# Two linear-attention branches with a gate: where x^T of the first 512 rows comes from, and where the gate is applied

## The chip, the core and the metric

The kernel runs on one core of a Trainium2 chip. The metric is device time in microseconds (us), as the median of several executions. A profile of one execution comes with it. Its engines are PE (TensorE: matmuls, and PEld its weight loads), DVE (VectorE), ACT (ScalarE), POOL (GpSimd) and SP, which here only issues DMAs.

## What is computed

Two attention branches A and B read the same x (2048 rows, 640 columns, 32 heads of 20), each with its own weights. A gate per row, from x and one vector, mixes them. Shapes and casts are left out:

```python
def branch(x, wqkv, wo):
    q, k, v = heads(x @ wqkv)
    phi = lambda t: jnp.where(t > 0, t + 1, jnp.exp(t)) + 1e-6
    pq, pk = phi(q), phi(k)
    kv = jnp.einsum("bhsd,bhse->bhde", pk, v)
    z = jnp.einsum("bhsd->bhd", pk)
    num = jnp.einsum("bhqd,bhde->bhqe", pq, kv)
    den = jnp.einsum("bhqd,bhd->bhq", pq, z)[..., None] + 1e-6
    return rows(num / den) @ wo

g = sigmoid((x * gate_w).sum(-1, keepdims=True))
out = g * branch(x, A_wqkv, A_wo) + (1 - g) * branch(x, B_wqkv, B_wo)
```

## The kernel before

The rows are cut into 16 tiles of 128, or 4 blocks of 512. x^T (tile XT, 640 columns as 5 chunks of 128 partitions) stands in SBUF, and so does x itself (XN, with a column of ones behind its 640 columns).

The work goes in stages. First k: for each row tile and branch, ten matmuls of 320 columns (`k_part`, XT against WK), then exp on ACT and two steps on DVE (`phi_k`) that leave phi(k). Then G = phi(k)^T [x | 1], 32 matmuls for each of five column groups and each branch (`g_unit`). ACT copies each G tile out, and SP transposes it by DMA (GTA, GTB). From G, WV and WO come small per-head matrices (`m_unit`) and the product with wo, WP (`wp_unit`, `wp_rows`). Then q: per block and branch five groups of five 512-column matmuls (`q_unit`) and the phi steps. `scale_q` makes the denominators of a block with twenty 32-wide matmuls of 256 columns, four of them side by side in the array (two halves of each branch), adds epsilon on DVE (DN, line 733), takes the reciprocal (RC), writes it to DRAM and reads it back repeated over the rows (RX), and multiplies phi(q) by it on DVE (line 757). Last, `final` multiplies phi(q) by WP: per row tile ten 320-column matmuls for A and ten for B.

The gate is applied in `final`. `gates` (line 654) takes sixteen products of x with the broadcast gate vector on DVE with a running sum (line 659), then exp on ACT, plus one and reciprocal on DVE: GA holds g and 1 - g for each row. In `final`, A's two PSUM banks are copied by ACT with scale g into TS (line 805), and DVE multiplies B's by 1 - g and adds TS (line 811). The last row tile is done in three column parts (320, 160, 160).

The order on each engine is made when the program is built: every operation has an estimated duration and its reads and writes, and `_Sched` places them one after the other on the engine that is free first, by order of writing among those that can start within 20 ns. DMAs stand in the queue of the engine that issues them, in the order in which they are written. `at[0]` chains the first matmuls, so that TensorE keeps their written order.

At the head, x^T of the first block is not loaded: rows 0 to 511 of x come as four loads of 128 rows, TensorE transposes each in five 128x128 steps with an identity that POOL builds (`transpose_x`, lines 472 to 482), and DVE copies the result to XT (line 486). Around them stand warm-up matmuls on ones, whose results nobody reads (`warm`: seven, then one after each of the first stretches). wk of A comes in five loads. ACT's queue issues wk chunks 0, 1, 2, 4 and x tile 3; SP's queue x tiles 0, 1, wk chunk 3, x tile 2, three loads of B's wk, then the DMA transposes of blocks 1 to 3 of x (512 rows each), the constants, the gate vector, x of blocks 1 to 3, and the other weights:

```python
load_wk("ACT", 0)
load_x("SP", 0)
load_wk("ACT", 1)
load_x("SP", 1)
load_wk("ACT", 2)
load_wk("SP", 3)
load_wk("ACT", 4)
load_x("SP", 2)
load_x("ACT", 3)
```

In the profile all matmuls but the transposes have line 396 (helper `mms`), and all DMAs line 385 (helper `dma`).

Of the kernel before, what the change touches and what calls it, by code (L numbers as in the profile page):

```python
# [14 lines left out]
dt = mybir.dt  # L15
# [4 lines left out]
D = 640  # L20
# [8 lines left out]
XW = 672  # L29
# [286 lines left out]
def bass_gated_mix__linear_attn_block__linear_attn_block__prompt_kernel(nc, A_x, A_wqkv, A_wo, B_x, B_wqkv, B_wo, gate_w, out):  # L316
# [6 lines left out]
    with ExitStack() as es:  # L323
# [24 lines left out]
        GL = sb("GL", [128, NT], dt.float32)  # L348
        GE = sb("GE", [128, 2, NT], dt.float32)
        GA = sb("GA", [128, 2, NT], dt.float32)  # L350
        GP = sb("GP", [128, D])
        GWB = sb("GWB", [128, D])
        NTS = 3
        TS = sb("TS", [128, NTS, D], dt.float32)
# [8 lines left out]
        IDN = sb("IDN", [128, 128])  # L363
# [40 lines left out]
        def wsrc(X, lo):  # L404
            return weights(X, lo, 0, NC)


        sch.op("POOL", lambda e: e.memset(IDN[:, :], 0.0), 150, writes=[("ID",)], name="id0")
        sch.op(
            "POOL",  # L410
            lambda e: e.affine_select(
                IDN[:, :], IDN[:, :], pattern=[[-1, 128]], compare_op=ALU.not_equal, fill=1.0, base=0, channel_multiplier=1
            ),
            400, writes=[("ID",)], name="id1",
        )
        def load_x(eng, t):
            dma(eng, "xn%d" % t, XN[:, t, 0:D], xin[128 * t : 128 * t + 128, :], writes=[("XN", t)], us=0.25)

        def load_wk(eng, c):
            dma(eng, "wkA%d" % c, WK["A"][:, c, :], weights("A", D, c, c + 1)[:, 0, :], writes=[("WK", "A", c)], us=0.25)  # L420

        load_wk("ACT", 0)
        load_x("SP", 0)
        load_wk("ACT", 1)
        load_x("SP", 1)
        load_wk("ACT", 2)
        load_wk("SP", 3)
        load_wk("ACT", 4)
        load_x("SP", 2)
        load_x("ACT", 3)  # L430
        for c0, c1 in ((0, 1), (1, 3), (3, 5)):
            dma(
                "SP", "wkB%d" % c0, WK["B"][:, c0:c1, :], weights("B", D, c0, c1), writes=[("WK", "B", c) for c in range(c0, c1)],
                us=0.55 * (c1 - c0),
            )
# [6 lines left out]
        dma("SP", "gw", GWB[:, :], gate_w.partition_broadcast(128), writes=[("GWB",)], us=0.4)  # L442
        for b in range(1, NB):
            dma(
                "SP", "xn_%d" % b, XN[:, 4 * b : 4 * b + 4, 0:D],
                xin[512 * b : 512 * b + 512, :].rearrange("(t p) f -> p t f", p=128),
                writes=[("XN", t) for t in range(4 * b, 4 * b + 4)], us=2.0,
            )
# [22 lines left out]

        def transpose_x(t):
            tt = _Tile(1)

            def fn(pe):
                ins = None
                for c in range(NC):
                    ins = pe.transpose(PSB[:, tt.banks[0], 128 * c : 128 * c + 128], XN[:, t, 128 * c : 128 * c + 128], IDN[:, :])  # L478
                return ins

            at[0] = sch.op(
                "PE", fn, 5 * 112, reads=[("XN", t), ("ID",)], writes=[(tt,)], name="xpose%d" % t, lat=190, after=at[0]
            )
            sch.op(
                "DVE",
                lambda e: e.tensor_copy(
                    XT[:, :, 128 * t : 128 * t + 128], PSB[:, tt.banks[0], 0:D].rearrange("p (c f) -> p c f", f=128)
                ),
                _dve_ns(D), reads=[(tt,)], writes=[("XT", t)], name="xev%d" % t,
            )  # L490

        ring = {"ek": _Ring(NEK), "dn": _Ring(2), "rx": _Ring(2), "os": _Ring(NOS), "ts": _Ring(NTS)}

# [160 lines left out]
        def gates():  # L654

            for t in range(NT):
                sch.op(
                    "DVE",
                    lambda e, t=t: e.scalar_tensor_tensor(  # L659
                        out=GP[:, :], in0=XN[:, t, 0:D], scalar=1.0, in1=GWB[:, :], op0=ALU.mult, op1=ALU.mult, accum_out=GL[:, t : t + 1]  # L660
                    ),
                    _dve_ns(D), reads=[("XN", t), ("GWB",)], writes=[("GL", t), ("GP",)], name="gl%d" % t,
                    after=gone["A"],
                )
            for x, sg in ((0, -1.0), (1, 1.0)):
                sch.op(
                    "ACT", lambda e, x=x, sg=sg: e.activation(GE[:, x, :], GL[:, :], ACT.Exp, scale=sg), _act_ns(NT, False),
                    reads=[("GL", t) for t in range(NT)], writes=[("GE", x)], name="ge%d" % x,
                )
            sch.op(  # L670
                "DVE", lambda e: e.tensor_scalar(GE[:, :, :], GE[:, :, :], 1.0, None, op0=ALU.add), 110, reads=[("GE", 0), ("GE", 1)],
                writes=[("GE", 0), ("GE", 1)], name="ge1",
            )
            sch.op(
                "DVE", lambda e: e.reciprocal(GA[:, :, :], GE[:, :, :]), 330, reads=[("GE", 0), ("GE", 1)], writes=[("GA",)], name="ga",
            )
# [35 lines left out]
        def scale_q(b, pieces):  # L712
# [4 lines left out]
            def den():  # L717
# [15 lines left out]
                lambda e: e.tensor_scalar(DN[:, ds.slot, :], PS[:, dtile.banks[0], 0:256], EPS, None, op0=ALU.add), _dve_ns(256),  # L733
                reads=[(dtile,)], writes=[(ds,)], name="dn%d" % b,
# [33 lines left out]
        def final(t, parts=((0, D),), put=None):  # L768

            last = len(parts) > 1  # L770
            os = None if last else _Tile(1, ring["os"])
            row = out[0, 128 * t : 128 * t + 128, :]
            for lo, hi in parts:
                n = 1 if hi - lo <= 512 else 2
                w = (hi - lo) // n
                ts = _Tile(1, ring["ts"])

                def o_ap(lo=lo, hi=hi, w=w):
                    v = OL[:, lo:hi] if last else OS[:, os.slot, lo:hi]
                    return v.rearrange("p (h f) -> p h f", f=w)  # L780

                def t_ap(ts=ts, hi=hi, lo=lo, w=w):
                    return TS[:, ts.slot, 0 : hi - lo].rearrange("p (h f) -> p h f", f=w)

                okey = ("OL", lo) if last else (os,)
                for x, X in enumerate(XS):
                    tile = _Tile(n)

                    def steps(X=X, tile=tile, lo=lo, w=w, n=n):
                        return [  # L790
                            (PS[:, tile.banks[h], 0:w], PQ[X][:, k, 128 * t : 128 * t + 128],
                             WP[X][:, k, lo + w * h : lo + w * h + w], k == 0, k == NC - 1, None)
                            for k in range(NC) for h in range(n)
                        ]

                    def acc(tile=tile, n=n, w=w):
                        b0 = tile.banks[0]
                        return PS[:, b0 : b0 + n, 0:w]

                    mms(  # L800
                        "f%s%d" % (X, t), steps, [("PQS", X, t)] + [("WP", X, k) for k in range(NC)], [(tile,)], 5 * n * (w + 6),
                    )
                    if x == 0:
                        sch.op(
                            "ACT", lambda e, acc=acc, t_ap=t_ap: e.activation(t_ap(), acc(), ACT.Copy, scale=GA[:, 0, t : t + 1]),  # L805
                            _act_ns(hi - lo), reads=[(tile,), ("GA",)], writes=[(ts,)], name="fa%d" % t,
                        )
                    else:
                        sch.op(
                            "DVE",  # L810
                            lambda e, acc=acc, t_ap=t_ap, o_ap=o_ap: e.scalar_tensor_tensor(  # L811
                                out=o_ap(), in0=acc(), scalar=GA[:, 1, t : t + 1], in1=t_ap(), op0=ALU.mult, op1=ALU.add
                            ),
                            _dve_ns(hi - lo), reads=[(tile,), (ts,), ("GA",)], writes=[okey], name="fb%d" % t,
                        )
                p0 = (put or {}).get(hi, None if last else 0)
                if p0 is not None:
                    outs.append(dma(
                        "SP", "out%d_%d" % (t, lo), row[:, p0:hi],
                        (lambda p0=p0, hi=hi: OL[:, p0:hi]) if last else (lambda: OS[:, os.slot, :]),  # L820
                        reads=[("OL", c) for c, _ in parts if p0 <= c < hi] if last else [(os,)], us=0.4,
                    ))
# [21 lines left out]
        for t in (2, 3):  # L844
            first("A", *[(t, c) for c in range(NC)])
            phi_k("A", t, kt["A", t])
# [81 lines left out]
```

## Time and profile before

| | us |
|---|---|
| three executions | 194.81, 195.17, 196.56 |
| median | 195.17 |
| the profiled execution | 194.81 |
| its span | 192.9 |
| first k matmul starts | 5.21 |
| k stage ends, G begins | 50 |
| first q matmul starts | 97.17 |
| last matmul ends, by the timeline | 190.26 |

A line of the profile has the source line, the engine, the operation and the tiles (out<-in) with their shapes. The timeline adds the start and the duration ahead of it, and in brackets how long the engine had been idle and what released it. A matmul's duration holds its way through the array, so that neighbours overlap: the distance between starts is the pace. Of a DMA the timeline shows the time that the issuing engine spends on it; the time from issue to landing is a figure of its own. Queue q1 is the one SP issues to, q10 that of ACT.

### The profile page before, as it was taken

The page shows a single profiled execution, that of the slowest core. Times are in us where ns is not written, and L with a number is a line of the kernel's source. Part 1 is how long each engine was busy: PE and PEld are TensorE (multiplying, and loading weights), DVE is VectorE, ACT ScalarE, POOL GpSimd, SP SyncE. Part 2 cuts the span into 40 slices and gives each one's busy share as a digit, 9 for nine tenths or more (in the row PEclk, how much of TensorE's full clock was granted, in tenths as well). Part 3 has the DMA queues.
Part 4 walks back from the last instruction along what each step waited for, and adds up shares of the span by engine and source line. Part 5 has one row for each costly group of instructions (what it writes and reads, how often), then busy time and mean ns, then how long its engine had stood idle before and what let it go on. Part 6 is the DMA issues. An engine that isn't in the chain of part 4 may idle for free.

```text
span 192.9 us, 3265 instructions
## 1 busy us (share of the span) xinstructions
PE 189.0 (98%) x1357; PEld 134.1 (70%) x1363; DVE 128.6 (67%) x249; ACT 73.6 (38%) x112; POOL 1.2 (1%) x9
## 2 busy tenths in 40 slices
PE   8999999999999999999999999999999999999994
PEld 3777777777888888888855665455675566777773
DVE  0298888888700009994179998999985997383323
ACT  2155554545211122103265377645224551332232
POOL 2000000000000000000000000000000000000000
PEclk9999999999999999999999999999999999999999
DMA  6999999994011511121155315352034000511112
GB/s 188 312 219 183 182 387 228 306 226 131 4 34 34 37 34 34 37 34 34 34 108 139 133 38 144 102 170 86 26 114 131 0 3 35 176 37 69 68 68 68
DMA packets 30609, 21.17 MB, mean 110 GB/s; under 512 B 15492, under 2 KB 30340, under 8 KB 30596
## 3 DMA queue, kind: packets, MB, share of 16 engines
q1 hardware_dynamic: 29876, 20.16, 41.0%
q10 hardware_dynamic: 720, 0.82, 1.2%
q8 instruction: 10, 0.16, 0.4%
q14 instruction: 3, 0.02, 0.0%
HBM read 12.06 MB, written 5.31 MB: 90 GB/s over the span
## 4 chain that ended last, share of the span: by engine, by line
PE 98%; issue 0%; ACT 0%; DVE 0%
PE ps L396 97%; PE ps L478 1%; ACT TS L805 0%; DVE OL L811 0%
## 5 line engine op out<-in xcount | busy, mean ns | idle before, releaser
L697 ACT ACTIVATE EK<-ps 128x512 bf16<-128x512 f32 x40 | 23.9, 597 | 21.2 <-PE ps L396 20.2
L504 ACT ACTIVATE EK<-ps 128x640 bf16<-128x640 f32 x32 | 22.4, 704 | 24.1 <-PE ps L396 24.1
L805 ACT ACTIVATE TS<-ps,GA 128x640 f32<-128x640 f32 (+2 forms) x18 | 13.2, 735 | 30.1 <-PE ps L396 30.1
L396 PE MATMUL ps<-WPA,FEA 128*128 128x320 bf16 (+1 forms) x165 | 24.7, 295 | 0.0
L396 PE MATMUL ps<-WPB,FEB 128*128 128x320 bf16 (+1 forms) x165 | 24.7, 295 | 0.0
L811 DVE SCALAR_TENSOR_TENSOR OS<-ps,GA,TS 128x640 bf16<-128x640 f32 x15 | 13.1, 876 | 15.7 <-PE ps L396 14.7
L396 PE MATMUL ps<-WKA,XT 128*128 128x320 bf16 x160 | 23.4, 303 | 0.0
L396 PE MATMUL ps<-XT,WQA 128*128 128x512 bf16 x95 | 22.4, 380 | 0.4 <-issue 0.2
L396 PE MATMUL ps<-XN,FEB 128*128 128x320 bf16 (+1 forms) x160 | 22.5, 300 | 0.0
L396 PE MATMUL ps<-WKB,XT 128*128 128x320 bf16 x160 | 22.4, 299 | 0.0
L396 PE MATMUL ps<-XT,WQB 128*128 128x512 bf16 x99 | 22.2, 379 | 0.1
L396 PE MATMUL ps<-XN,FEA 128*128 128x320 bf16 (+1 forms) x160 | 22.0, 300 | 0.0
L555 ACT ACTIVATE GS<-ps 128x640 bf16<-128x640 f32 x10 | 7.0, 704 | 37.1 <-PE ps L396 37.1
L396 PEld LDWEIGHTS ps<-XN,FEA 128*128 128x128 bf16 x160 | 18.8, 117 | 3.0
L396 PEld LDWEIGHTS ps<-XN,FEB 128*128 128x128 bf16 x160 | 18.7, 118 | 2.9
L396 PEld LDWEIGHTS ps<-WPA,FEA 128*128 128x128 bf16 x165 | 15.8, 98 | 6.5 <-issue 0.4
L396 PEld LDWEIGHTS ps<-WKA,XT 128*128 128x128 bf16 x160 | 15.8, 99 | 6.2
L396 PEld LDWEIGHTS ps<-WPB,FEB 128*128 128x128 bf16 x165 | 15.9, 98 | 5.9
L396 PEld LDWEIGHTS ps<-WKB,XT 128*128 128x128 bf16 x160 | 15.7, 98 | 6.1
L396 PEld LDWEIGHTS ps<-XT,WQB 128*128 128x128 bf16 x100 | 11.7, 117 | 9.7
L396 PEld LDWEIGHTS ps<-XT,WQA 128*128 128x128 bf16 x100 | 11.4, 118 | 8.9 <-issue 0.7
L659 DVE SCALAR_TENSOR_TENSOR GP<-XN,GWB 128x640 bf16<-128x640 bf16 x16 | 13.3, 834 | 4.1 <-PE ps L396 3.6
(49 smaller groups left out, 152.6 us busy)
## 6 DMA issues: line engine op xcount, KB each, us to landing
out_dram<-OS SPq DMA_DIRECT2D x15, 160.0 KB, 1.8
XN<-in_A_x_dram SPq DMA_DIRECT2D x3, 640.0 KB, 8.3
factor<-RC SPq DMA_DIRECT2D x4, 256.0 KB, 2.6
RX<-factor SPq DMA_DIRECT2D x4, 256.0 KB, 2.7
WVA<-in_A_wqkv_dram SPq DMA_DIRECT2D x1, 800.0 KB, 11.9
WQA<-in_A_wqkv_dram SPq DMA_DIRECT2D x1, 800.0 KB, 14.1
WVB<-in_B_wqkv_dram SPq DMA_DIRECT2D x1, 800.0 KB, 16.9
WQB<-in_B_wqkv_dram SPq DMA_DIRECT2D x1, 800.0 KB, 14.1
```

The costliest lines, as they stand in the source:

```text
L396: ins = pe.matmul(o, l, r, start=a, stop=z, tile_position=tp, skip_group_check=True)
L478: ins = pe.transpose(PSB[:, tt.banks[0], 128 * c : 128 * c + 128], XN[:, t, 128 * c : 128 * c + 128], IDN[:, :])
L504: "ACT", lambda e: e.activation(ek2(), pair(tile, HALF), ACT.Exp),
L555: "ACT", lambda e: e.activation(GS[:, k, :].rearrange("p (h f) -> p h f", f=HALF), pair(tile, HALF), ACT.Copy),
L659: lambda e, t=t: e.scalar_tensor_tensor(out=GP[:, :], in0=XN[:, t, 0:D], scalar=1.0, in1=GWB[:, :], op0=ALU.mult, op1=ALU.mult, accum_out= ...
L697: "ACT", lambda e: e.activation(ek(), PS[:, tile.banks[0], :], ACT.Exp), _act_ns(512), reads=[(tile,)],
L805: "ACT", lambda e, acc=acc, t_ap=t_ap: e.activation(t_ap(), acc(), ACT.Copy, scale=GA[:, 0, t : t + 1]),
L811: lambda e, acc=acc, t_ap=t_ap, o_ap=o_ap: e.scalar_tensor_tensor(out=o_ap(), in0=acc(), scalar=GA[:, 1, t : t + 1], in1=t_ap(), op0=ALU.m ...
```

## The change

x^T of the first block now comes by DMA too: four transposes of 128 rows each, the first entries of SP's queue, ahead of the three of 512 rows. The identity, the transposes on TensorE and the copies on DVE are gone. All of wk (five loads for A, two for B) is issued by ACT. x of the first block joins the later loads of x, as a fourth one of 512 rows, since G still reads it. The warm-up matmuls stay nine, but stand elsewhere: after the seven, one after the first two k matmuls and one after the next six.

The gate moves from the output rows into the denominators. Twenty 32-wide matmuls of 512 columns (the gate vector repeated over 32 columns against XT, four side by side) put x . gate_w of every row on 32 partitions; ACT takes exp with sign - for A and + for B into UG (eight pieces), POOL adds one, and DVE's step on the denominators multiplies by UG: (den + eps) * (1 + exp(-+l)), whose reciprocal is the gate over the denominator. So `final` sums A and B in one pair of PSUM banks, and ACT alone copies them out. The scheduler writes the gate's matmuls right behind the five G groups of A. XN's row pitch goes from 672 to 642.

```diff
-XW = 672
+XW = 642
...
-        load_wk("ACT", 0)
-        load_x("SP", 0)
...
+        for t in range(4):
             dma(
+                "SP", "xt0_%d" % t, XT[:, :, 128 * t : 128 * t + 128], xin[128 * t : 128 * t + 128, :], writes=[("XT", t)], us=1.0,
+                transpose=True,
+            )
+        for c in range(NC):
+            dma("ACT", "wkA%d" % c, WK["A"][:, c, :], weights("A", D, c, c + 1)[:, 0, :], writes=[("WK", "A", c)], us=0.25)
+        for c0, c1 in ((0, 2), (2, NC)):
+            dma(
+                "ACT", "wkB%d" % c0, WK["B"][:, c0:c1, :], weights("B", D, c0, c1), writes=[("WK", "B", c) for c in range(c0, c1)],
+                us=0.5 * (c1 - c0),
             )
...
-        dma("SP", "gw", GWB[:, :], gate_w.partition_broadcast(128), writes=[("GWB",)], us=0.4)
-        for b in range(1, NB):
+        dma("SP", "gw", GWC[:, :], gate_w.rearrange("(c p) -> p c", p=128), writes=[("GWC",)], us=0.4, slow=True)
+        for b in range(NB):
...
         def gates():
...
+            sch.op(
+                "POOL", lambda e: e.tensor_copy(GW[:, :, :], GWC[:, :].unsqueeze(2).to_broadcast([128, NC, H])), 400,
+                reads=[("GWC",)], writes=[("GW",)], name="gwb",
+            )
+            tile = _Tile(1)
+
+            def steps():
+                r = []
+                for c in range(NC):
+                    xs = XT[:, c, :].rearrange("p (b g f) -> p b g f", g=4, f=128)
+                    for g in range(4):
+                        r.append((
+                            PS[32 * g : 32 * g + 32, tile.banks[0], :].rearrange("p (b f) -> p b f", f=128), GW[:, c, :], xs[:, :, g, :],
+                            c == 0, c == NC - 1, (0, 32 * g),
+                        ))
+                return r
+
+            mms("gate", steps, [("GW",)] + [("XT", t) for t in range(NT)], [(tile,)], 5 * 560)
             for x, sg in ((0, -1.0), (1, 1.0)):
+                for g in range(4):
+                    to = 32 * (2 * x + g // 2)
+                    sch.op(
+                        "ACT",
+                        lambda e, to=to, g=g, sg=sg: e.activation(
+                            UG[to : to + 32, :, 128 * (g % 2) : 128 * (g % 2) + 128],
+                            PS[32 * g : 32 * g + 32, tile.banks[0], :].rearrange("p (b f) -> p b f", f=128), ACT.Exp, scale=sg,
+                        ),
+                        _act_ns(512), reads=[(tile,)], writes=[("UG", x, g)], name="ug%d%d" % (x, g),
+                    )
+            sch.op(
+                "POOL", lambda e: e.tensor_scalar(UG[:, :, :], UG[:, :, :], 1.0, None, op0=ALU.add), _pool_ns(1024),
...
-                lambda e: e.tensor_scalar(DN[:, ds.slot, :], PS[:, dtile.banks[0], 0:256], EPS, None, op0=ALU.add), _dve_ns(256),
+                lambda e: e.scalar_tensor_tensor(
+                    out=DN[:, ds.slot, :], in0=PS[:, dtile.banks[0], 0:256], scalar=EPS, in1=UG[:, b, :], op0=ALU.add, op1=ALU.mult,
+                ),
...
+        def final(t):
+            tile = _Tile(2)
+            os = _Tile(1, ring["os"])
...
+            sch.op(
+                "ACT", lambda e: e.activation(OS[:, os.slot, :].rearrange("p (h f) -> p h f", f=HALF), pair(tile, HALF), ACT.Copy),
+                _act_ns(D), reads=[(tile,)], writes=[(os,)], name="oe%d" % t,
+            )
...
+        def final_parts(t):
+            row = out[0, 128 * t : 128 * t + 128, :]
+            for lo, hi, eng, put in ((0, 320, "ACT", 0), (320, 480, "DVE", None), (480, D, "ACT", 320)):
...
         warm(7)
-        transpose_x(0)
+        first("A", (0, 0))
         warm(1)
-        transpose_x(1)
-        first("A", (0, 0), (0, 1))
+        first("A", (0, 1), (1, 0), (1, 1))
         warm(1)
-        first("A", (1, 0), (1, 1))
-        first("A", (0, 2), (1, 2), (0, 3), (1, 3))
-        transpose_x(2)
+        first("A", *[(t, c) for c in (2, 3) for t in (0, 1)])
         for t in (0, 1):
             first("A", (t, 4))
             phi_k("A", t, kt["A", t])
```

## Prediction

> **What bounds the kernel now.** I read the busy times first, then the chain of work that ended last, then the timeline of the first 12 us and of the last 5, and last the DMA traffic of the first 9 us. From the page, busy time by engine and the chain's shares by engine:
>
> ```profile
> PE 189.0 (98%) x1357; PEld 134.1 (70%) x1363; DVE 128.6 (67%) x249; ACT 73.6 (38%) x112; POOL 1.2 (1%) x9
> ...
> PE 98%; issue 0%; ACT 0%; DVE 0%
> ```
>
> TensorE works nearly all the span and is 98% of the chain. The chain's "issue" pieces (0.04, 0.18, 0.07, four of 0.05, 0.02) sum to about 0.5 us: relief of DVE or ACT can win no more. So three things count: matmuls added or removed, waits at the head, the steps after the last matmul. The timeline of the head (start, duration, what):
>
> ```profile
> 0.78 3.15 PE L396 MATMUL ps<-const-bfloat16-1.0 128*128 128x512 bf16 x7 [0.78 <-PEq L913]
> ...
> 3.71 0.74 PE L478 MATMUL ps<-IDN,XN 128*128 128x128 bf16 x5
> 4.05 13.22 SPq L385 DMA_TRANSPOSE XT<-in_A_x_dram  x3
> ...
> 5.21 1.27 PE L396 MATMUL ps<-WKA,XT 128*128 128x320 bf16 x4
> ...
> 6.28 0.43 PE L396 MATMUL ps<-const-bfloat16-1.0 128*128 128x512 bf16 x1
> ...
> 6.54 1.79 PE L396 MATMUL ps<-WKA,XT 128*128 128x320 bf16 x12
> ...
> 9.28 2.88 PE L396 MATMUL ps<-WKA,XT 128*128 128x320 bf16 x20
> ...
> 11.99 5.60 PE L396 MATMUL ps<-WKB,XT 128*128 128x320 bf16 x40
> ```
>
> See two things. TensorE never waits for data: seven warm-ups end as the first x rows land at 3.64 (issued 0.74, 2.9 to landing). And its pace changes: the first four 320-column matmuls start 0.267 us apart ((6.28-5.21)/4); after the warm-up at 6.28 they run at 0.136 ((5.60-0.30)/39). The pace doubles about 6.3 us, 5.5 after the first matmul. The 20 matmuls of rows 256 to 511 begin at 9.28: this is my mark, for after it nothing on TensorE waits.
>
> **The change part by part.** All sums start from the profiled execution: 194.81 us, a span of 192.90 and 1.91 around it. It is the fastest of three, 0.36 below their median 195.17.
>
> *Gate matmuls, on the path.* Twenty 32-wide matmuls of 512 columns come right after A's G matmuls. The nearest row is the denominator:
>
> ```profile
> 110.37 0.29 PE L396 MATMUL ps<-FEA,ZBDA 128*32 128x256 bf16 x2
> 110.37 0.29 PE L396 MATMUL ps<-FEB,ZBDB 128*32 128x256 bf16 x2
> 110.49 0.28 PE L396 MATMUL ps<-FEA,ZBDA 128*32 128x256 bf16 x2
> ...
> 110.81 0.28 PE L396 MATMUL ps<-FEA,ZBDA 128*32 128x256 bf16 x2
> ...
> 111.06 0.48 PE L396 MATMUL ps<-WOB,MB 120*120 120x320 bf16 x2
> ```
>
> Four run at once; five groups take 110.37 to 111.06 = 0.69, that is 5 x 0.11 + 0.14. At 512 columns a matmul of q starts every 0.216 ((5.56-0.38)/24 in the stretch from 102.34), so 5 x 0.216 + 0.14 = **+1.22**. Ends: 1.08 without the switch, 4.3 if all twenty run one by one; the denominator row is nearest.
>
> *What hides the gate's rest.* Eight ACT exponentials of 32x512: 8 x 0.597 (the 128x512 row) = 4.8 us. Seven stand ahead of the copy of B's first G tile, 4.2 us, while that tile needs 32 x 0.136 = 4.35: hidden by 0.15, and another PSUM pair covers a slip. POOL adds one to 1024 elements; its nearest row, 128 elements in 0.29, makes 2.3 us, and the first reader runs at 111.5, some 30 us later. Widening the gate column on POOL waits for its small DMA, about 20 us before use. All zero; 0.6 (one exponential) if the cover is gone.
>
> *DVE and the output rows.* Sixteen gate products (13.3 us) and fifteen row merges (13.1 us) leave DVE. The output matmuls stay 320 columns and as many; A and B now accumulate in one pair of banks, emptied once by ACT (0.79 per row tile against 20 x 0.136 = 2.7 of matmuls). Zero, at best -0.5 (the issue pieces).
>
> *The end.* Before:
>
> ```profile
> 189.75 0.51 PE L396 MATMUL ps<-WPB,FEB 128*128 128x160 bf16 x5
> 189.95 0.39 ACT L805 ACTIVATE TS<-ps,GA 128x160 f32<-128x160 f32 x1 [0.30 <-PE ps L396]
> 190.38 0.38 DVE L811 SCALAR_TENSOR_TENSOR OL<-ps,GA,TS 128x160 bf16<-128x160 f32 x1 [0.31 <-ACT TS L805]
> ```
>
> The last matmul ends at 190.26, DVE at 190.76. Now one ACT copy follows: 0.04 + 0.39 = 0.43 instead of 0.50: **-0.07**. The row pitch 672 to 642: the M matmuls already read moving columns at odd offsets at full pace (30 in 1.59 us), so zero.
>
> *Later loads.* SP issues four small transposes, then three of 512 rows. In this trace a 128-row transpose (GTA) holds SP 1.20 us and lands 2.6 after issue; a 512-row one holds it 3.25. So the first 512-row issue moves from 4.05 to 0.74 + 4 x 1.2 = 5.55, but has no 1.5 MB of plain loads ahead, which had stretched it to 6.33 on SP; it lands by about 11 (the last one landed 5.5 after issue), and is needed at 17. The constants, the gate load (640 tiny elements instead of 160 KB) and four x loads follow; the last x load landed near 29 and is needed at 50, the weights from 75 on. Zero. ACT issues seven loads instead of five, 0.9 us longer, ahead of its table load (3.10 to 4.4 us); the first exponential ran at 8.93. Zero.
>
> *The head, the term that decides.* Out go 20 transposes, 0.53 + 0.53 + 0.28 + 0.28 = 1.62 of the chain. In comes a wait: the first k matmul needs tile t0, the fifth needs t1. SP ends the four issues at 1.95, 3.15, 4.35 and 5.55, and the copies of GTA show data only after SP's part is done. The engines are shared with seven weight loads, 1.64 MB, on the other queue. How is shown by the DMA traffic of two windows, 3 to 5 us and 6 to 7 us (packets, MB, share), both queues loaded with 1280-byte rows:
>
> ```profile
> q1 hardware_dynamic: 306, 0.34, 55.4%
> q10 hardware_dynamic: 325, 0.37, 50.4%
> ```
>
> ```profile
> q1 hardware_dynamic: 160, 0.18, 54.0%
> q10 hardware_dynamic: 162, 0.19, 51.2%
> ```
>
> Packet for packet. A transpose's packets are 256 bytes (550 of them in 0.14 MB while one GTA copy ran), a weight row's 1280. On one of 16 engines a small one takes 256 B / (290 GB/s / 16) = 14 ns, the rate of the 512-row transposes; a large one 1280 / (390 / 16) = 52 ns. If they alternate, 640 packets of a tile, 40 on each engine, take 40 x 66 ns = 2.65 us. t0: 1.95 + 2.65 + 0.45 (last data to landing, as GTA) = 5.05. The weights end near 1.75 + 80 x 0.066 = 7.0, t1 with them: 7.6. t2 and t3 follow alone, 8.2 and 8.8. The other end is no contention: landing 2.0 after SP's part, as the last 512-row transpose (17.25 to 19.2): 3.94, 5.15, 6.36, 7.55.
>
> TensorE at the slow end: idle from 3.71 to 5.05, two matmuls, a warm-up and two more to 6.54, idle to 7.6, then 16 matmuls and a warm-up. At full pace that is 16 x 0.136 + 0.22 = 2.4, the mark at 10.0: +0.7. If the pace doubles 5.5 us after the restart at 5.05, at 10.55, then 2.95 us pass at the slow pace (a warm-up 0.43 and 9.4 matmuls), 6.6 more take 0.9: mark 11.45, +2.2. If it counts from 7.6, all is slow, 4.7 us, mark 12.3, and three matmuls more: +3.4. At the free end: start 3.98, 8 matmuls and a warm-up to 6.41, then 0.22 + 12 x 0.136: mark 8.26, -1.0. I take the alternation, since the packet counts show it, and half way between its first two paces: **+1.45**.
>
> Sum: 194.81 + 1.45 + 1.22 - 0.07 = **197.4**.
>
> Two rules beside this. The Trainium skill, "DMA: Bandwidth & Descriptors", Queues, rings and completion order, says that an engine switches between queues after a whole packet; the counts agree, and whether a transpose's 256 bytes are such a packet no row shows. The page "VectorE: DVE Perf Modes", Rules for kernel authors, speaks against the change: transpose 128x128 on TensorE where PSUM will do; its table gives 1309 ns by DMA. By an estimate from that page five blocks take 6.5 us, t1 comes at 0.74 + 13 = 13.8 and the time is about 203; the GTA copies, 2.6 us for five blocks, decide against the figure.
>
> **The rivals.**
> - *The transposes are not held up* (bytes shared evenly, or weights soon done). For it: a weight load's rows wait on memory too, and DMA is at 0.87 from 5 to 6 us. The head wins 1.0: 194.81 - 1.02 + 1.22 - 0.07 = 194.9, not slower than before. It decides if t1 lands by about 5.4.
> - *In between*: t0 4.6, t1 6.3. At full pace the mark is 8.7 (-0.6), 195.4; with the slow pace to 10.1 (4.6 + 5.5) it is near 10.6 (+1.3), 197.3.
> - *The pace starts anew after the second wait*: +3.4, 199.4. For it: the trace shows one doubling, after 5.5 us without a gap. Against it: the gap is only 1.06 us.
> - *The gate's matmuls don't overlap*: +3.1 on any of these, 198 to 202.5. Against it: the denominator rows.
> - *Relief of DVE shows*: -0.5 on any; against it the PE share of 98%.
>
> **How the numbers follow.** Alternating 0.30 (around 197.4, 196.6 to 198.2); pace anew 0.18; not held up 0.24; in between 0.23; gate in series 0.03; something else that wins, as a cheaper head with no issue pieces, 0.02. 1% is 1.95 us, about what a measurement of this kernel can tell from no change; against 195.17 the bounds are 193.2 and 197.1. Slower: 0.6 of the first, all of the second, a third of the in-between, the gate: 0.18 + 0.18 + 0.08 + 0.03, about 0.47. Faster: 0.03. Same: 0.50. The range 194.4 to 199.8 reaches 0.5 and 0.4 past the first and the fourth case, for the trace's gaps and the unknown moment of the doubling; it leaves out the gate in series and some 0.07 at each end. The point lies just over the 1% bound, so "same" and "slower" are near each other.
>
> **What would show it.** The first matmul on WKA near 5.0 (rival: 4.0) with TensorE idle before it, the fifth near 7.6 (5.2); the mark between 10 and 11.5 (8.3); 20 matmuls on GW in 1.2 us; from the mark on, equal stretches but for the gate. Wrong would be a wait of TensorE anywhere after the mark, or transposes that land more than 2.7 us apart.

## The result, and the profile after

The changed kernel takes 201.31 us (median of 6, 199.96 to 201.65) against 194.81 for the kernel before (median of 6). The ratio is 1.0315, with a 95% interval of 1.0262 to 1.0369: slower by 6.1 us (the medians stand 6.5 apart). The prediction said 197.4, within 194.4 to 199.8. One execution of the runs below (204.2 us, wk in half rows) was in a slower state and is left out of medians and ratios.

The profiled execution took 201.55 us with a span of 199.8. Its page has, by engine, the busy time, and by engine and by line the chain that ended last:

```profile
PE 191.7 (96%) x1357; PEld 133.5 (67%) x1363; DVE 101.2 (51%) x194; ACT 76.1 (38%) x117; POOL 3.8 (2%) x9
...
PE 94%; DMA 4%; SPq 1%; issue 0%; ACT 0%
PE ps L391 94%; DMA XT<-in_A_x_dram 4%; SPq L380 1%; ACT OL L785 0%
```

DVE lost 27 us of work and the time didn't fall. What is new in the chain is a DMA: the small transposes into XT. TensorE's timeline of the head shows where it waits (start, duration, what, idle before):

```profile
0.76 3.14 PE L391 MATMUL ps<-const-bfloat16-1.0 128*128 128x512 bf16 x7 [0.76 <-PEq L881]
4.92 0.45 PE L391 MATMUL ps<-WKA,XT 128*128 128x320 bf16 x2 [1.02 <-DMA XT<-in_A_x_dram]
5.21 0.38 PE L391 MATMUL ps<-const-bfloat16-1.0 128*128 128x512 bf16 x1
5.42 0.43 PE L391 MATMUL ps<-WKA,XT 128*128 128x320 bf16 x2
9.22 1.25 PE L391 MATMUL ps<-WKA,XT 128*128 128x320 bf16 x4 [3.36 <-DMA XT<-in_A_x_dram]
10.26 0.63 PE L391 MATMUL ps<-const-bfloat16-1.0 128*128 128x512 bf16 x1
10.69 6.50 PE L391 MATMUL ps<-WKA,XT 128*128 128x320 bf16 x32
17.03 3.15 PE L391 MATMUL ps<-WKB,XT 128*128 128x320 bf16 x22
```

Tile t0 comes at 4.9 and t1 at 9.2: two waits, 1.02 and 3.36 us. Then the pace is slow again. The matmuls that begin at 9.22 stand 0.26 us apart, and so they go on; the same thing as TensorE's granted clock, the column after the busy counts in the table by stretches:

```profile
7.00:8.00 1.00, 0.00 (x0) 0.00 (x0) 0.00 (x0) 0.00 (x0) 0.00 (x0) 0.96 1.10 138
8.00:9.00 1.00, 0.00 (x0) 0.00 (x0) 0.00 (x0) 0.00 (x0) 0.00 (x0) 0.50 1.26 140
9.00:10.00 1.00, 0.78 (x4) 0.44 (x5) 0.00 (x0) 0.00 (x0) 0.00 (x0) 0.50 1.02 272
...
13.00:14.00 1.00, 1.00 (x6) 0.56 (x4) 0.00 (x0) 0.40 (x1) 0.00 (x0) 0.50 1.32 215
14.00:15.00 1.00, 1.00 (x7) 0.58 (x6) 0.63 (x2) 0.90 (x2) 0.00 (x0) 0.63 1.27 290
15.00:16.00 1.00, 1.00 (x10) 0.73 (x8) 0.97 (x3) 0.13 (x1) 0.00 (x0) 1.00 0.98 202
```

The pace had doubled by 5.2; in the gap that follows the clock falls to one half at 7.9, and comes back only at 14.7. Ahead of its first change the column doesn't tell the pace: it shows 1.00 at 1 to 4 us too, where seven warm-ups of 512 columns take 3.14 us, the slow pace. The last column is the DMA traffic in GB/s, and it is low just where TensorE waits. The Trainium skill, "TensorE: Matmul & The Clock Gate", Part 1, says that an idle window of some 3.4 us puts the half clock back and a busy one lifts it. The half clock agrees; here it fell 2.1 us into a gap of 3.36, stayed for 6.8 us and was lifted 5.5 us after the restart.

The DMA traffic from 6 to 9 us, first before, then after (the line with packets, megabytes and mean rate, then by queue):

```profile
DMA packets 1018, 1.10 MB, mean 366 GB/s; under 512 B 178, under 2 KB 1018, under 8 KB 1018
...
q1 hardware_dynamic: 781, 0.84, 81.7%
q10 hardware_dynamic: 237, 0.26, 24.2%
```

```profile
DMA packets 878, 0.42 MB, mean 140 GB/s; under 512 B 680, under 2 KB 878, under 8 KB 878
...
q10 hardware_dynamic: 219, 0.25, 80.4%
q1 hardware_dynamic: 659, 0.17, 37.4%
```

A packet on q10, nearly always a weight row of 1280 bytes, now takes 0.804 x 3 us x 16 / 219 = 176 ns; before, it took some 50 (24.2% for 237, 81.7% for 781). The two shares after sum to 118%: an engine can have more than one packet under way, so 176 ns is the time of a packet on record and not the engine's alone. The transposes' packets are three to one of the rows, not one to one. In the window of before nearly all is plain loads; 178 small packets are in it. Plain loads were slow once without transposed data beside them: in the kernel before, from 5 to 6 us, 201 GB/s with 13 small packets among 170. Another execution with the same head (old head, new gate, below) moved 347 there.

Behind the head, G's matmuls on x, before and then after, and in the kernel after also the gate's:

```profile
50.02 21.96 PE L396 MATMUL ps<-XN,FEA 128*128 128x320 bf16 x160
```

```profile
55.06 22.30 PE L391 MATMUL ps<-XN,FEA 128*128 128x320 bf16 x160
77.29 1.26 PE L391 MATMUL ps<-XT,GW 128*32 128x512 bf16 x20
78.49 9.05 PE L391 MATMUL ps<-XN,FEB 128*128 128x320 bf16 x64
```

The gate takes 77.29 to 78.49 = 1.20. But A's 160 G matmuls take 0.34 longer: (22.30 - 0.30)/159 = 0.1384 each instead of 0.1362. The end of the kernel after:

```profile
196.78 0.51 PE L391 MATMUL ps<-WPB,FEB 128*128 128x160 bf16 x5
197.32 0.30 ACT L785 ACTIVATE OL<-ps 128x160 bf16<-128x160 f32 x1 [0.94 <-PE ps L391]
```

The bill between the two profiled spans: the first matmul on B's wk moves from 11.99 to 17.03, +5.04. From there to the last matmul's end, 180.26 instead of 178.27: +1.99, of which 1.20 is the gate, 0.68 G (twice 0.34), 0.11 spread over the rest. From the last matmul to the end of the span 2.51 instead of 2.64: -0.13. Sum 6.90 = 199.8 - 192.9.

### The profile page after: what moved, and what is told of

Its sections match the earlier page's. It is cut to its first block, busy times and chain, and to the rows that moved or that the text cites. A ratio compares the mean times of both kernels' runs of the same rounds, so it can differ in the third digit from the quotient of the medians.

```text
span 199.8 us, 3206 instructions
## 1 busy us (share of the span) xinstructions
PE 191.7 (96%) x1357; PEld 133.5 (67%) x1363; DVE 101.2 (51%) x194; ACT 76.1 (38%) x117; POOL 3.8 (2%) x9
## 4 chain that ended last, share of the span: by engine, by line
PE 94%; DMA 4%; SPq 1%; issue 0%; ACT 0%
PE ps L391 94%; DMA XT<-in_A_x_dram 4%; SPq L380 1%; ACT OL L785 0%
## 5 line engine op out<-in xcount | busy, mean ns | idle before, releaser
L391 PE MATMUL ps<-WKA,XT 128*128 128x320 bf16 x160 | 25.4, 320 | 4.4 <-DMA XT<-in_A_x_dram 4.4
L391 PEld LDWEIGHTS ps<-WKA,XT 128*128 128x128 bf16 x160 | 16.5, 104 | 13.3 <-DMA XT<-in_A_x_dram 5.6
L759 ACT ACTIVATE OS<-ps 128x640 bf16<-128x640 f32 x15 | 10.6, 704 | 31.9 <-PE ps L391 31.9
L466 DVE TENSOR_SCALAR EK<-EK 128x640 bf16<-128x640 bf16 x32 | 10.4, 326 | 19.3 <-ACT EK L462 19.3
L391 PEld LDWEIGHTS ps<-XT,WQA 128*128 128x128 bf16 x100 | 11.4, 118 | 8.9 <-issue 0.7
L675 DVE SCALAR_TENSOR_TENSOR FEB<-ps,EK 128x512 bf16<-128x512 f32 x20 | 13.4, 688 | 0.3
```

Of the source, the lines that this page charges most:

```text
L391: ins = pe.matmul(o, l, r, start=a, stop=z, tile_position=tp, skip_group_check=True)
L466: "DVE", lambda e: e.tensor_scalar(ek(), ek(), 1.0, EPS, op0=ALU.min, op1=ALU.add), _dve_ns(D, 4),
L675: lambda e: e.scalar_tensor_tensor(out=dst, in0=PS[:, tile.banks[0], :], scalar=0.0, in1=ek(), op0=ALU.max, op1=ALU.add),
L759: "ACT", lambda e: e.activation(OS[:, os.slot, :].rearrange("p (h f) -> p h f", f=HALF), pair(tile, HALF), ACT.Copy),
```

## The experiments

Theory: plain weight loads on one queue and transposes on the other slow each other, the waits cost TensorE its pace as well, and gate and row pitch add their own. Rivals: small transposes at the head are slow in any company; the pace has nothing to do with the gap; the parts don't add up to the whole. Ratios are against the kernel before in the same rounds. "B starts" is the first matmul on B's wk in the one profile of each: 11.99 before, 17.03 after. That column scatters: 11.86 to 12.14 in four profiles with the old head (mean 12.0), 15.14 to 17.03 in five with the new (mean 16.1), so that a difference of less than about 2 us between single profiles with the new head says little, unless its parts are followed in the trace.

| run | ratio [95%] | median us | B starts |
|---|---|---|---|
| old head, new gate | 1.0062 [1.0036, 1.0088] | 196.25 | 11.86 |
| the same, pitch 672 | 1.0038 [1.0012, 1.0065] | 195.99 | 12.12 |
| before, pitch 642 | 1.0024 [0.9998, 1.0051] | 195.66 | 12.14 |
| new head alone | 1.0188 [1.0145, 1.0230] | 198.76 | 16.02 |
| new head alone, again | 1.0176 [1.0130, 1.0223] | 198.49 | 15.14 |
| after, again | 1.0279 [1.0232, 1.0326] | 200.37 | 15.58 |
| after, pitch 672 | 1.0294 [1.0258, 1.0330] | 200.21 | 16.62 |
| after, 16 warm-ups in the gap | 1.0301 [1.0241, 1.0361] | 200.72 | 16.28 |
| after, 8 warm-ups in the gap | 1.0252 [1.0210, 1.0294] | 200.06 | 15.22 |
| after, wk behind the transposes | 1.1220 [1.1177, 1.1262] | 218.18 | |
| after, wk in half rows, first build | 1.1056 [1.1010, 1.1102] | 215.01 | |
| after, wk in half rows | 1.0336 [1.0289, 1.0384] | 201.74 | 17.21 |
| after, B's wk behind | 1.0239 [1.0198, 1.0280] | 200.04 | 15.47 |
| after, one queue | 1.0211 [1.0151, 1.0271] | 198.85 | 14.04 |
| before, tiles 2 and 3 by DMA | 0.9957 [0.9935, 0.9979] | 193.89 | 11.10 |

In "wk in half rows", "B's wk behind" and "one queue" the gate's matmuls are also made to wait for A's G matmuls, where they stand in the kernel after. Without that the late wk let the scheduler put them ahead of the k stage or into it, where they waited for the gate load; this is what the times of "wk behind the transposes" and of the first build show, and these two are used for the landings alone.

### The whole taken apart

Old head with the new gate: the loads, identity, transposes and order of the head as before, the rest as after.

> The head of the kernel before (x rows loaded, transposed on TensorE, wk on both queues) with everything else of the kernel after: gate in the denominators, pitch 642. Theory (head +5.0, gate +1.2, pitch +0.65, end -0.1): 1.75 above the kernel before, about 196.6 beside 194.8. Rival (the gate's part is free, all is the head): within 0.4 of before.

> As the run with the old head and the new gate, but with the pitch of x at 672. Theory: the pitch gives 0.65 back, 1.1 above the kernel before, about 195.9: the gate's matmuls alone, less 0.1 at the end. Rival (the pitch does nothing): as the run before it, 1.75 above.

Measured +1.2 us (0.62% of 194.9) and, with pitch 672, +0.7 (its median 1.1 above that of before), somewhat less than the 1.75 and 1.1 expected. The gate does cost about a microsecond and is not free; in its profile the twenty matmuls take 1.2 us again.

```diff
-XW = 672
+XW = 642
```

> The kernel before with the pitch of x at 642 elements and nothing else. Theory: ten G tiles 0.06 to 0.07 us longer each, 0.65 above before, about 195.5. Rival (the slower G tiles come of the change's other parts): no difference, G tiles at 4.36.

The time is +0.5, its interval just touching none; the profile settles it, as nothing else differs. G's matmuls of that kernel, with the pace of the kernel after:

```profile
50.18 22.30 PE L396 MATMUL ps<-XN,FEA 128*128 128x320 bf16 x160
```

> Kernel after with the row pitch of XN back at 672 elements (1344 bytes) instead of 642 (1284). Theory (the pitch slows the reads of x by the G matmuls): a G tile's 32 matmuls take 4.36 us as before instead of 4.42 to 4.43, ten tiles 0.65 us less, about 200.6. Rival (the 0.7 us in the G stage come from the later ACT copies or the gate): the G tiles keep 4.42, no change.

The median is 1.1 below that of after, but the ratios, 1.0294 and 1.0315, can't be told apart. The G matmuls are back at the old pace: A's 160 take 21.96 us again, instead of 22.30. So by the traces the pitch is 0.7 us of the whole.

> The kernel before with the head of the kernel after alone: four small transposes by DMA, all wk on ACT's queue, no transposes on TensorE; gates per output row and pitch 672 stay. Theory: the head is worth +5.0, so about 199.8. Rival (the head and the gate's loads and matmuls disturb each other, so that parts don't add): below 198.5 or above 201.

The new head alone is worth +3.7, less than the +5.0 read from one trace. Here the pace had not doubled before the gap; it did so at 12.8, where the profile of after had the full clock back at 14.7. Run again, with the kernel after on the same chip:

> The kernel after again, beside the new head alone on the same chip. If the parts add: after is 1.2 to 1.4 us above the new head alone (the old head with the new gate had 1.2 above before). If they interact: 2.5 us above it, as in the separate runs.

> The new head alone again (gates per output row, pitch 672), beside the kernel after on the same chip. If the earlier 198.8 was typical: 198.3 to 199.3. If the moment the pace doubles decides, it scatters up to 200 or more.

After is 1.0279 [1.0232, 1.0326], the new head alone 1.0176 [1.0130, 1.0223]: 1.9 us apart, between the two answers, and the new head did not scatter to 200. The product 1.0062 x 1.0176 = 1.0239 lies just inside this interval of the whole; with the first run of the new head it is 1.0251, just below the first interval (1.0262 to 1.0369). So the parts add to within about a microsecond; whether that much is left over by an interaction, these runs can't tell. In this second profile of after B starts at 15.58, 1.45 sooner than in the first: t1 landed at 8.3 instead of 9.2, and the head differs that much from one execution to the next.

### Are the transposes slow, or their company?

All seven wk loads wait for t3:

```diff
-dma("ACT", "wkA%d" % c, ..., writes=[("WK", "A", c)], us=0.25)
+dma("ACT", "wkA%d" % c, ..., reads=[("XT", 3)], writes=[("WK", "A", c)], us=0.25)
```

> Kernel after, but all seven wk loads wait until the fourth small transpose of x has landed, so the four transposes run with nothing beside them. Theory (the weight loads on the other queue hold the transposes up): tiles t0 to t3 land as SP issues them, 1.2 to 1.3 us apart, near 3.9, 5.2, 6.5 and 7.8 instead of 4.9, 9.2 and later. Rival (the small transposes of DRAM rows are slow by themselves at the head): they land some 4 us apart as in the kernel after, the last past 12. The whole time says less, since wk now comes late: first matmul near 10 by the theory, near 15 by the rival.

Alone, t0, t1 and t2 landed 2.8, 2.8 and 3.0 us after issue, near 3.6, 4.9 and 6.4, and ACT could issue the first wk load at 8.49, after t3 (expected at 7.8; the first transpose of 512 rows was behind it by then). In the kernel after it was 4.2, 7.1, 7.4 and 9.1 (4.9, 9.2, 10.8 and 13.8). For t1, in the kernel after and then alone:

```profile
DMA to landing us min/median/max: 7.1/7.1/7.1
```

```profile
DMA to landing us min/median/max: 2.8/2.8/2.8
```

The theory holds and the rival falls. The traffic of this run from 0 to 8 us, transposes only, at a glance: busy tenths of the DMA engines in 40 slices:

```profile
DMA  0000000000199930025996003499700169940363
```

It comes in four bursts with gaps. SP's issuing (1.25 to 1.33 us each), not the engines, paces the transposes when nothing else runs. From 6 to 9 us a packet of a transpose took 22 ns in this run (64.6% for 1405), and 27 in the kernel after (37.4% for 659), so it is the weight rows that the company slows most.

Each wk load in two column halves, 640-byte packets:

> Kernel after with every wk load split into two column halves: the same bytes in packets of 640 B instead of 1280, twice as many. Theory (queues take turns packet for packet): each turn of a weight row is half as long, t1 lands earlier, by 6.5 to 8 instead of 9.2, if 5.5 to 9 us are limited by turns. Rival (bytes are shared, or the mix of small and large reads is slow whatever the turns): t1 lands at 9.2 or later. Time 199.5 to 200.5 by the theory, 201 or more by the rival.

> Kernel after with every wk load in two column halves (packets of 640 B instead of 1280), and the gate's matmuls held behind A's G matmuls, where they stand in the kernel after. An earlier look at the same loads had t0 to t3 land 4.2, 4.4, 4.6 and 4.6 us after issue, against 4.2, 7.1, 7.4 and 9.1 with whole rows. Theory (the mix of transposes and long weight rows makes the wait): t1 lands near 6.5, the mark comes at 10.5 to 11.5 instead of 13.9, the time is 198 to 199.5. Rival (the head's cost is the clock, not the landing): 201.

The transposes came 4.2, 4.3, 4.7 and 4.9 us after issue, t1 near 6.4: the first part of the expectation holds. But the time did not fall, 201.74. The waits changed owners:

```profile
8.24 1.95 PE L391 MATMUL ps<-WKA,XT 128*128 128x320 bf16 x8
11.47 3.42 PE L391 MATMUL ps<-WKA,XT 128*128 128x320 bf16 x24 [1.29 <-DMA WKA<-in_A_wqkv_dram]
17.21 5.59 PE L391 MATMUL ps<-WKB,XT 128*128 128x320 bf16 x40 [2.32 <-issue]
```

From 6 to 9 us the engines moved 207 GB/s, more than 140, still far from 366; a packet on q10 took 47 ns (51.8% for 527) instead of 176. Smaller packets shift who is held up; the head has 2.3 MB to bring either way, and at some 200 GB/s that takes 11 us. Two more things changed, so this run doesn't show what the packet size alone does: ACT needs until 8.03 to issue the twelve loads, instead of 4.78 for seven, so that less was under way beside the transposes, and each of B's two loads now holds half of the columns of all rows, so that B's first matmul needs both.

B's wk on SP behind the four transposes:

> Kernel after with the two loads of B's wk on SP's queue behind the four small transposes, so that only A's wk runs beside them. Theory 1 (the slump to 140 GB/s from 6 to 9 us comes from A's rows as much as from B's): t1 still lands near 9, only t2 and t3 come sooner, 200.5 to 201.3. Theory 2 (B's loads, with 256 and 384 rows each, make the slump): t1 lands near 6 to 7, 198.5 to 199.5.

t1 landed at 8.0 and t3 at 9.2 instead of 13.8, 229 GB/s from 6 to 9 us, ratio 1.0239. It lies between the two expectations: A's rows beside the transposes hold t1 up, B's do the rest. After t1 TensorE waited for no tile in this profile, but its pace doubled only near 12.7, so part of this run's time is pace.

All on SP's queue, in the order t0, t1, A's wk, t2, t3, B's wk:

> Kernel after with all loads of the head on SP's queue, one after the other: tiles t0 and t1, A's wk in five loads, t2 and t3, B's wk in two; no wk on ACT. Theory (two kinds of transfer beside each other from two queues are slow): t0 and t1 land 2.8 to 3.5 us after issue, near 3.5 and 5.0, as when they run alone; A's wk follows by 7 to 8; no traffic near 140 GB/s; the first matmul on B's wk at 12 to 13.5 instead of 17, the time 196.5 to 198. Rival (a transpose at the head is slow in any order): t1 lands at 7 or later, wk after it, the time 201 or more.

t0 and t1 landed 3.1 and 3.0 us after issue, so order alone makes them fast, and the rival fell a second time. The gain is less than expected (198.85, 1.5 below the kernel after in the same rounds, B at 14.04): now A's wk is late, and the first k matmul waits for it.

```profile
6.50 0.43 PE L391 MATMUL ps<-WKA,XT 128*128 128x320 bf16 x2 [2.60 <-DMA WKA<-in_A_wqkv_dram]
```

The pace fell again, 1.3 us after that wait had ended and while TensorE worked: 32 matmuls from 8.18 need 6.03 us. The stretches have the clock in the column behind the busy counts:

```profile
7.00:8.00 1.00, 1.00 (x8) 0.67 (x7) 0.00 (x0) 0.00 (x0) 0.00 (x0) 0.92 0.93 247
8.00:9.00 1.00, 1.00 (x5) 0.48 (x4) 0.00 (x0) 0.00 (x0) 0.00 (x0) 0.50 1.16 176
```

And 228 GB/s from 6 to 9 us shows that the two kinds in one queue, where they follow each other, also don't reach 366.

### What the slow pace is worth

Warm-up matmuls in the gap before t1:

```diff
-first("A", (0, 1), (1, 0), (1, 1))
+first("A", (0, 1))
+warm(16)
+first("A", (1, 0), (1, 1))
```

> Kernel after with sixteen more warm-up matmuls (results unread) in the gap between the fourth and the fifth k matmul, where TensorE waits from 5.85 to 9.2 for tile t1. Theory (the wait costs twice: the gap itself, and the slow pace that follows it until 14.5): TensorE stays at full pace, the mark (first matmul of rows 256 to 511) comes at 11.5 to 12 instead of 13.9 and no slow matmuls follow: 2.2 to 2.9 us less, 198.4 to 199.1. Rival (the slow pace is no result of the gap, but of DMA or of the time since the start): pace still halves, the same 201 or up to 0.5 more.

A miss: 200.72. In that profile the pace had not yet doubled when the warm-ups began, they took 4.9 us instead of 3.4 and ended at 11.2, 2 us after t1 was there. With eight:

> Kernel after with eight warm-up matmuls in the gap ahead of the fifth k matmul; sixteen had run 6.3 to 11.2, two us past the landing of t1. Theory (the slow pace follows from the gap): the eight fill 6.3 to 9.5, the pace has doubled by then, the mark comes near 11.7 and nothing slow follows: 2 us less than after, about 199.2. Rival (busy or not, the pace is slow until 14): mark at 14, 201.3.

```profile
6.04 1.91 PE L391 MATMUL ps<-const-bfloat16-1.0 128*128 128x512 bf16 x8
8.97 0.72 PE L391 MATMUL ps<-WKA,XT 128*128 128x320 bf16 x4 [1.03 <-DMA XT<-in_A_x_dram]
9.53 0.38 PE L391 MATMUL ps<-const-bfloat16-1.0 128*128 128x512 bf16 x1
9.74 3.17 PE L391 MATMUL ps<-WKA,XT 128*128 128x320 bf16 x22
13.85 1.53 PE L391 MATMUL ps<-WKA,XT 128*128 128x320 bf16 x10 [0.94 <-DMA XT<-in_A_x_dram]
15.22 5.60 PE L391 MATMUL ps<-WKB,XT 128*128 128x320 bf16 x40
```

The gap shrinks to 1.03, the pace stays full, and the mark stands at 9.74 + 12 x 0.136 = 11.4, as expected. Of the 2.5 us won there, 0.94 goes to the next late tile, t3: 1.8 at B's start. A second way gives the same: in the first profile of after t3 landed at 13.8, and its ten matmuls at full pace would have ended at 15.2, not 17.0. So of the head's 5.0 in that profile about 1.8 is pace; the rest is waiting for transposes, less the 1.62 of TensorE's own that fell away. In time the eight warm-ups won less than the 2 us expected, 1.25 between the medians, 0.5 against the second run of after, and the intervals overlap: the gain is seen in the trace and not clear of the noise in the time.

The pace differs from one execution to the next. Of the six of the result four have a mean granted clock of 0.983, as the profiled one, whose 6.8 us at half make just that, and spans of 198.9 to 199.8; two have 1.000, with 198.2 and 198.7. A mean of 1.000 is no proof of full pace: the second profile of after has it too, and its pace doubled only near 12.7. And the length of the wait alone doesn't set the moment: in four profiles in which the clock had risen early (after, after with pitch 672, new head again, one queue) it fell at 7.7 to 7.9, whether the wait was 2.0, 2.5, 2.6 or 3.4 us long, and was half for 6.8, 6.8, 3.4 and 3.4 us. That such a wait costs pace is shown; what sets the moment is not.

### A version that beats both

The kernel before, with tiles 2 and 3 alone by DMA, behind two x loads and one of wk on SP's queue:

```diff
-        load_x("SP", 2)
-        load_x("ACT", 3)
+        for t in (2, 3):
+            dma("SP", "xt0_%d" % t, XT[:, :, 128 * t : 128 * t + 128], xin[128 * t : 128 * t + 128, :], ..., transpose=True)
...
-        transpose_x(2)
...
-        transpose_x(3)
```

> The kernel before with x^T of tiles 2 and 3 alone by DMA, on SP's queue behind two x loads and one wk load, ahead of B's wk; tiles 0 and 1 stay on TensorE. The transposes then run when most plain loads ahead are done. Theory: they land by 8.2 and 9.5, in time, and TensorE is free of two transposes of 0.28 us: 0.3 to 0.6 less than before, 194.3 to 194.6. Rival (any transpose beside plain loads at the head comes late): a wait of 1 us or more at the mark, 196 or more.

Ratio 0.9957 [0.9935, 0.9979], 0.8 us less than before. The head:

```profile
5.20 0.95 PE L396 MATMUL ps<-WKA,XT 128*128 128x320 bf16 x4
5.99 0.38 PE L396 MATMUL ps<-const-bfloat16-1.0 128*128 128x512 bf16 x1
6.21 5.05 PE L396 MATMUL ps<-WKA,XT 128*128 128x320 bf16 x36
11.10 5.60 PE L396 MATMUL ps<-WKB,XT 128*128 128x320 bf16 x40
```

The two tiles landed at 6.7 and 7.4, ahead of their use at 8.4 and 9.7, and TensorE never waits. (x of these rows, which G still reads, comes in one plain load behind the constants.) B starts 0.89 sooner: 0.56 are the two transposes, the rest is a pace that in this execution doubled a little earlier. Here A's wk was nearly through when the transposes' data came: from 5.25 us on, when they fill the engines, 29 of the 576 packets of ACT's queue were left, and B's wk stood behind the transposes on their own queue. 302 GB/s flowed from 6 to 9 us.

## Why the prediction was wrong

The term that failed is the head: +1.45 in the sum, +5.04 in the profile, +3.4 and +3.7 in the two runs of the new head alone. Two of its steps were wrong, and a third term, put at zero, was not zero.

*Wrong: the landing of the tiles.* The step was "if they alternate, 640 packets of a tile, 40 on each engine, take 40 x 66 ns", with each packet at the time that it takes among its own kind. It gave t0 5.05, t1 7.6, t2 8.2, t3 8.8; measured were 4.9, 9.2, 10.8, 13.8, so the first came out right and the others did not. Neither half holds: a weight row beside transposes takes 176 ns, not 52, and the queues did not take turns one to one. Why the mix is so slow stays open. The rival of a slow transpose in itself falls too: alone they land 2.8 to 3.0 us after issue, as the GTA row had it. The two equal packet counts in the trace of before, both of plain rows, said nothing of a mix. "Transposes that land more than 2.7 us apart" was named as what would make the prediction wrong, and it came.

*Wrong: the pace.* The mean between two cases, +1.45, left out what the rival named: the pace starting anew, +3.4. With a second gap of 3.36 us instead of 1.06 that rival is what happened, in the first profile at its worst (slow until 14.7). The rows of before could not tell when the clock falls, since TensorE never paused there.

*Wrong: the row pitch, "so zero".* The M matmuls with odd column offsets were no row for a pitch of 1284 bytes; it costs 0.0022 us a matmul, 0.7 in all.

*Right:* the gate's matmuls, 1.20 for 1.22, four at a time; its exponentials and POOL's addition (2.77 us, 30 us ahead of use) hidden; DVE's relief worth nothing; the end, -0.13 for -0.07; nothing of the later loads was late.

*Beside the trace stands the skill.* "Advanced Engine Details and Errata", X-Bar Transpose (TRN2), says that transposing DMAs are as fast as plain ones. Here a transpose of 512 rows alone moves 290 GB/s (after, 14 to 15 us), and plain loads 366; the measurement decides. Of the two kinds side by side, which move 140 GB/s here, that sentence says nothing.

## What to carry to other kernels

A DMA's price read from a trace holds for its company: ask what else is in flight where the step will stand, and take mixed traffic from a run, not from the sum of two pure rates. At a head that TensorE waits for, place the transposes behind the plain loads that come first, and leave to TensorE the tiles that are needed before those are through. A wait of 2 to 3 us on TensorE can cost a second time in pace, so look at the distance between matmul starts behind every wait.

## What the runs showed of the hardware that was not expected

- Plain loads of 1280-byte rows on one queue and DMA transposes (256-byte packets) on another moved 140 GB/s together from 6 to 9 us; plain rows nearly alone 366; with 640-byte rows, which were also issued later, 207. Why the long rows take 176 ns instead of some 50 was not tried further.
- x with a row pitch of 1284 bytes instead of 1344 slows each 320-column matmul that streams it from 0.1362 to 0.1384 us.
- TensorE's pace first doubled at 4.8 to 6.7 us with the old head, where it works without a break, and with the new head and its waits by 5 to 6.5, at 9.1 (wk in half rows, and with sixteen warm-ups), or only at 12.7 to 12.9. Where it rose early, the granted clock fell to half again at 7.7 to 7.9, after or in a wait of 2.0 to 3.4 us, once while TensorE had been at work for 1.3 us, and stayed there for 3.4 or 6.8 us.
